# The last chunk's output stores: one SyncE transfer with two row groups in place of a SyncE and a ScalarE transfer

## The chip, the cores and the metric

The kernel runs on one core of a Trainium2 chip (trn2). The metric is the device time of one execution in microseconds, taken as the median over several runs. A profiled execution of its own gives the trace; its span is somewhat shorter than the time of the runs, since it counts from the first to the last instruction.

## The reference

Forgetting attention (causal, with a decay that is the cumulated log of a forget gate), then an MLP with exact gelu over all tokens. Batch 8, heads 8, sequence 576, head size 64, so 4608 tokens of 512 channels; the MLP goes from 512 to 2048 and back.

```python
# q, k, v [8, 8, 576, 64], f [8, 8, 576]; w_in [512, 2048], w_out [2048, 512]
scores = q @ k.T / sqrt(64)
cum = cumsum(log(clip(f, 1e-4, 1.0)))
decay = cum[:, :, :, None] - cum[:, :, None, :]
attn = softmax(where(causal, -1e9, scores + decay)) # "causal" is the part above the diagonal
x = (attn @ v).transpose(0, 2, 1, 3).reshape(4608, 512)
h = x @ w_in
out = (0.5 * h * (1 + erf(h / sqrt(2)))) @ w_out # float32 [4608, 512]
```

## The kernel before

The program works through the 8 batches, each with attention, a first matmul (`gemm1`, 512 to 2048, with gelu on ScalarE) and a second one (`gemm2` and its variants, 2048 to 512). A batch has 576 tokens, but `gemm1` and `gemm2` take 512 tokens at a time, as four blocks of 128 tokens. So the MLP runs over nine chunks: chunks 0 to 7 are the first 512 tokens of each batch, and chunk 8, the last, holds the 64 remaining tokens ("tails") of all eight batches. The tile `tails` collects them.

The order on each engine is that in which the program issues its instructions. For chunks 0 to 6 the second matmul is woven into the attention of a later batch (`gemm2_rows`, `gemm2_half`), and their stores go through `store` (L480 to L481). Chunk 7 and chunk 8 use `gemm2` (L394 on). Lines L728 to L731 are the end of the program: `gemm2` of chunk 7, then sixteen calls of `gemm1` on the tails, then `gemm2` of chunk 8.

In `gemm2` each token block `ts` accumulates sixteen matmuls in one PSUM bank (L408). The last block of chunk 8 is done in two column parts, 384 and then 128 columns (L398 to L403), so that the first part can be copied and stored while the second is computed. When a part is finished, VectorE copies it to an SBUF tile `ot` (L416 to L417). The pool of these tiles, `o_pool`, has four buffers; chunk 8 takes five of them, one for each block and one more for the last block's second part.

The store (L418 to L426) depends on the chunk. In chunks 0 to 7 the 128 tokens of a block are consecutive rows of the output, so it is one transfer on SyncE's queue. In chunk 8 a block of 128 partitions holds the 64 last tokens of one batch and the 64 last tokens of the next. In the output these two groups are 576 rows apart. The kernel before makes two transfers of 64 rows each: partitions 0 to 63 on SyncE's queue, partitions 64 to 127 on ScalarE's. The four blocks give five parts in all (three whole blocks and two column parts), so ten transfers.

`P` is 128, `S` is 576, `TC` is 512, `TL` is 64, `B` is 8, `d_model` is 512.

Of the kernel before, what the change touches and what calls it, by code (L numbers as in the profile page):

```python
# [14 lines left out]
P = 128  # L15
S = 576
# [5 lines left out]
TC = 512  # L22
# [30 lines left out]
def kernel(  # L53
# [10 lines left out]
    nc = tc.nc  # L64
# [8 lines left out]
    TL = S - TC  # L73
# [63 lines left out]
    for t, op, fill in (  # L137
# [4 lines left out]
            out=t[0:D],  # L142
# [251 lines left out]
    def gemm2(c):  # L394

        whole = (0, d_model)
        order = [(ts, kt, whole) for ts in range(n_sub) for kt in range(n_ff)]
        if c == B:  # L398
            order[-n_ff:] = [
                (n_sub - 1, kt, part)  # L400
                for part in ((0, 3 * P), (3 * P, d_model))
                for kt in range(n_ff)
            ]  # L403
        pss = {}
        for ts, kt, (c0, c1) in order:
            if kt == 0:
                pss[ts] = m_psum.tile([P, d_model], FP32, tag="m", name="ps2")
            nc.tensor.matmul(  # L408
                pss[ts][:, c0:c1],
                g_of[c][kt][:, ts * P : (ts + 1) * P],  # L410
                w_out_sb[:, kt, c0:c1],
                start=(kt == 0),
                stop=(kt == n_ff - 1),
            )
            if kt == n_ff - 1:
                ot = o_pool.tile([P, d_model], FP32, tag="ot", name="ot")  # L416
                nc.vector.tensor_copy(ot[:, c0:c1], pss[ts][:, c0:c1])  # L417
                if c < B:  # L418
                    at = [(c * S + ts * P, 0, P)]
                else:  # L420
                    b0 = P // TL * ts
                    at = [(b * S + TC, (b - b0) * TL, TL) for b in range(b0, b0 + P // TL)]
                for row, p0, n in at:
                    (nc.scalar if p0 else nc.sync).dma_start(
                        out[row : row + n, c0:c1], ot[p0 : p0 + n, c0:c1]
                    )  # L426
            yield


# [268 lines left out]
    for b in range(B):  # L698
# [8 lines left out]
        for ffb in range(0 if b > 1 else 4, n_ff):  # L707
# [11 lines left out]
            elif b + 1 < B:  # L719
                first, gap = (5, 3) if b == 1 else (0, 4)  # L720
                at, late = divmod(ffb - first, gap)
# [4 lines left out]
                if ffb == (9 if b == 1 else 14):  # L726
                    load_qk_tokens(b + 2)
    take(gemm2(B - 1), 999)  # L728
    for ffb in range(n_ff):
        gemm1(B, ffb)  # L730
    take(gemm2(B), 999)  # L731


# [28 lines left out]
```

The softmax here doesn't subtract the row's maximum and nothing guards it: scores larger than these inputs give would overflow.

## Time and profile before

| | us |
|---|---|
| median of 3 runs | 345.75 (345.21 to 346.38) |
| span of the profiled execution | 343.4 |
| TensorE busy | 328.6 (96%) |
| ScalarE busy | 212.3 (62%) |
| VectorE busy | 187.0 (54%) |
| GpSimd busy | 124.2 (36%) |
| last gelu on ScalarE begins | 325.9 |
| matmuls of chunk 8's `gemm2` | 325.8 to 339.7 |

Each row of the profile's table of groups is one line of the program on one engine. In the timeline a row has its start in the span, its length, the engine, the line, the operation, the tile written and read, and how many instructions it covers. `SPq` and `ACTq` mark instructions that issue DMAs from SyncE and ScalarE; these aren't counted as busy time. In the DMA view, the lines "DMA" and "GB/s" cut the window into 40 equal slices: a digit is the mean busy share of the core's 16 DMA engines in tenths. The lines of queues below it (q1 is that of SyncE, q10 that of ScalarE) give packets, megabytes, and the time that the packets took as a share of 16 engines over the window. The list of issues gives a transfer's size and its time from issue to landing, that is, to the last of its semaphore increments.

### The profile page before, as it was taken

What the parts mean: (1) busy time and instruction counts of PE and PEld (TensorE: products, weight loads), DVE (VectorE), ACT (ScalarE), POOL (GpSimd) and SP (SyncE); (2) the same over time, 40 slices, a digit from 0 to 9 for tenths busy, and PEclk for the clock granted to TensorE, in tenths of its full rate; (3) what the DMA queues carried; (4) which work ended last, traced back from release to release, by engine and by line L of the source; (5) the groups of instructions that cost most, each with busy time, mean ns of one, the idle gap of its engine ahead of it and who ended that gap; (6) DMA issues with size and microseconds to landing.
All of it is one profiled execution on the core that took longest, in us unless ns stands there. A gap on an engine that the chain in (4) does not pass through costs nothing.

```text
span 343.4 us, 7895 instructions
## 1 busy us (share of the span) xinstructions
PE 328.6 (96%) x3182; PEld 174.7 (51%) x3227; DVE 187.0 (54%) x424; ACT 212.3 (62%) x296; POOL 124.2 (36%) x256
## 2 busy tenths in 40 slices
PE   7799999999999999999999999999999999999995
PEld 3574555445554456545654565446544654444443
DVE  5660355933467935796479646974597542020011
ACT  5986786773644787368746874687468755504600
POOL 8390672228328034543445243714261430000000
PEclk9999999999999999999999999999999999999999
DMA  8999999989993999578945896499900230011013
GB/s 117 178 176 194 201 166 153 170 158 148 237 184 102 139 192 188 82 101 165 211 121 73 141 212 139 71 160 198 169 31 2 65 88 31 2 61 61 0 38 87
DMA packets 99924, 43.03 MB, mean 125 GB/s; under 512 B 78704, under 2 KB 95344, under 8 KB 99888
## 3 DMA queue, kind: packets, MB, share of 16 engines
q1 hardware_dynamic: 82592, 28.37, 41.4%
q0 software_dynamic: 16896, 13.63, 27.2%
q8 instruction: 25, 0.41, 0.5%
q10 hardware_dynamic: 400, 0.52, 0.4%
q14 instruction: 11, 0.09, 0.1%
HBM read 36.85 MB, written 9.44 MB: 135 GB/s over the span
## 4 chain that ended last, share of the span: by engine, by line
PE 89%; issue 2%; POOL 2%; DVE 2%; ACT 2%; DMA 2%; POOLq 0%; ACTq 0%; DVEq 0%
PE ps L375 36%; PE ps L466 25%; PE o L320 9%; PE ps L408 8%; PE s L289 7%; PE ps L501 2%; ACT e L299 2%; DMA k<-in_k_dram 2%; PE ps_x L353 1%; DVE x L334 1%; POOL q L107 1%; PE ps_f L206 1%; POOL k L107 1%; DVE r L333 0%; DVE xT L356 0%
## 5 line engine op out<-in xcount | busy, mean ns | idle before, releaser
L392 ACT ACTIVATE g<-ps 128x512 bf16<-128x512 f32 x144 | 85.3, 597 | 81.1 <-PE ps L375 81.1
L299 ACT ACTIVATE e<-s 128x896 bf16<-128x896 f32 (+2 forms) x128 | 101.2, 836 | 28.5 <-PE s L289 26.8
L375 PE MATMUL ps<-xT,w_in_sb 128*128 128x512 bf16 x497 | 111.4, 379 | 0.8
L466 PE MATMUL ps<-w_out_sb,g 64*128 64x512 bf16 (+1 forms) x731 | 103.0, 376 | 0.8 <-issue 0.8
L375 PEld LDWEIGHTS <-w_in_sb 128*128 128x128 bf16 x576 | 56.0, 98 | 67.5 <-issue 1.8
L301 POOL TENSOR_SCALAR_AFFINE_SELECT e<-e 128x256 bf16<-128x256 bf16 (+1 forms) x135 | 49.2, 383 | 98.9 <-ACT e L299 98.6
L466 PEld LDWEIGHTS <-g 64*128 64x128 bf16 (+1 forms) x756 | 41.5, 94 | 40.4 <-issue 11.9
L244 DVE COPY qT<-tq 64x288 bf16<-64x288 bf16 x96 | 48.7, 507 | 1.4
L289 PE MATMUL s<-qT,kT 64*128 64x320 bf16 (+4 forms) x384 | 45.8, 276 | 3.6 <-ACT e L299 2.7
L260 POOL TENSOR_TENSOR vw<-v_sb,wT 128x640 bf16<-128x640 f32 x31 | 39.6, 1278 | 23.5 <-DMA v_sb<-in_v_dram 23.3
L320 PE MATMUL o<-vw,e 128*128 128x65 bf16 x960 | 36.8, 194 | 3.5 <-issue 2.4
L474 DVE COPY ot<-ps 128x512 f32<-128x512 f32 x26 | 17.9, 689 | 37.1 <-PE ps L466 35.2
L320 PEld LDWEIGHTS <-e 128*128 128x128 bf16 x960 | 34.8, 98 | 5.3 <-PE ps_x L353 0.3
L244 DVE COPY kT<-tk 64x288 bf16<-64x288 bf16 x96 | 33.0, 343 | 1.6
L334 DVE TENSOR_TENSOR x<-o,r 128x320 bf16<-128x320 f32 x64 | 31.4, 491 | 2.4 <-DVE r L333 0.2
L417 DVE COPY ot<-ps 128x512 f32<-128x512 f32 (+2 forms) x9 | 5.7, 632 | 48.8 <-PE ps L408 31.9
L289 PEld LDWEIGHTS <-kT 64*128 64x128 bf16 x384 | 19.5, 94 | 23.2 <-issue 9.7
L408 PE MATMUL ps<-w_out_sb,g 128*128 128x512 bf16 (+2 forms) x142 | 27.9, 355 | 0.1
L333 DVE RECIPROCAL r<-o 128x5 f32<-128x5 f32 x64 | 12.1, 189 | 27.6 <-PE o L320 27.5
L408 PEld LDWEIGHTS <-g 128*128 128x128 bf16 x144 | 13.5, 98 | 14.5
L476 DVE TENSOR_TENSOR ot<-ot,ps 128x512 f32<-128x512 f32 x26 | 17.9, 687 | 1.5
L365 POOL COPY tails<-xT 128x256 bf16<-128x256 bf16 x8 | 3.2, 399 | 31.3 <-DVE xT L356 31.3
(64 smaller groups left out, 158.1 us busy)
## 6 DMA issues: line engine op xcount, KB each, us to landing
out_dram<-ot SPq DMA_DIRECT2D x32, 256.0 KB, 2.3
v_sb<-in_v_dram SPq DMA_DIRECT2D x24, 256.0 KB, 5.3
q<-in_q_dram POOLq DMA_DIRECT2D x6, 576.0 KB, 6.1
k<-in_k_dram POOLq DMA_DIRECT2D x6, 576.0 KB, 8.2
v_sb<-in_v_dram SPq DMA_DIRECT2D x22, 128.0 KB, 5.1
w_in_sb<-in_moe_w_in_dram POOLq DMA_DIRECT2D x4, 512.0 KB, 6.7
w_out_sb<-in_moe_w_out_dram POOLq DMA_DIRECT2D x4, 512.0 KB, 8.4
q<-in_q_dram POOLq DMA_DIRECT2D x4, 144.0 KB, 4.6
```

Source lines behind the costliest of these rows:

```text
L244: nc.vector.tensor_copy(rows[:, odd], src[odd * D : (odd + 1) * D, 2 * i + h].rearrange("d j p -> d p j"),)
L260: eng.tensor_tensor(vw_of[b][:, hs, :, 0:D], v_sb[:, hs, :, :], w.unsqueeze(3).to_broadcast([P, 2, NBLK, D]), Alu.mult,)
L289: nc.tensor.matmul(to, *ab, start=half < 0, stop=half == 1 or not masked)
L299: nc.scalar.activation(et[:, :, z:c], st[:, :, z:c], Act.Exp, scale=scale)
L301: nc.gpsimd.affine_select(out=et[:, :, c0 + z : c0 + P], in_=et[:, :, c0 + z : c0 + P], compare_op=Alu.is_ge, fill=0.0, base=z, pattern=[[ ...
L320: nc.tensor.matmul(o[:, m, :], e_of[b, i, t][:, h, c : c + P], vw_of[b][:, 2 * i + h, n, :], start=(n == 0), stop=(n == m),)
L334: nc.vector.tensor_tensor(x_of[b, i][:, :, h, :], o[:, :, 0:D], r.unsqueeze(2).to_broadcast([P, NBLK, D]), Alu.mult,)
L375: nc.tensor.matmul(ps, w_in_sb[:, kt, ffb * P : (ffb + 1) * P], src[:, kt, 0:TC], start=(kt == 0), stop=(kt == n_dm - 1),)
L392: nc.scalar.activation(g_of[c][ffb], ps, Act.Gelu)
L408: nc.tensor.matmul(pss[ts][:, c0:c1], g_of[c][kt][:, ts * P : (ts + 1) * P], w_out_sb[:, kt, c0:c1], start=(kt == 0), stop=(kt == n_ff - 1),)
L466: nc.tensor.matmul(banks[r], g_of[c][kt][rows, ts * P : (ts + 1) * P], w_out_sb[rows, kt, :], start=kt == (steps.index("r") if r else 0), ...
L474: nc.vector.tensor_copy(ot, banks[1])
```

## The change

The last chunk's store becomes one SyncE transfer for each finished part. Its output side is a view of the output with the batch as a dimension of its own: [2 batches, 64 rows, columns] where the source is [128 partitions, columns]. The transfers of chunks 0 to 7 stay as they were, written in another form.

```diff
                 ot = o_pool.tile([P, d_model], FP32, tag="ot", name="ot")
                 nc.vector.tensor_copy(ot[:, c0:c1], pss[ts][:, c0:c1])
                 if c < B:
-                    at = [(c * S + ts * P, 0, P)]
+                    to = out[c * S + ts * P : c * S + (ts + 1) * P, c0:c1]
                 else:
                     b0 = P // TL * ts
-                    at = [(b * S + TC, (b - b0) * TL, TL) for b in range(b0, b0 + P // TL)]
-                for row, p0, n in at:
-                    (nc.scalar if p0 else nc.sync).dma_start(
-                        out[row : row + n, c0:c1], ot[p0 : p0 + n, c0:c1]
-                    )
+                    to = out.rearrange("(b s) d -> b s d", s=S)[
+                        b0 : b0 + P // TL, TC:S, c0:c1
+                    ]
+                nc.sync.dma_start(to, ot[:, c0:c1])
             yield
```

## The prediction

> **What bounds the kernel now.** I read the chain of waits first, cut to the last 18 us, because every instruction of the change is issued there.
>
> ```profile
> by line: PE ps L408 72.7%; PE ps L375 4.8%; DVE ot L417 1.5%; issue 0.4%
> ...
> 329.11 10.58 PE ps L408 x64
> 339.69 0.02 issue
> 339.71 0.29 DVE ot L417
> ```
>
> Columns are start, length, what. TensorE runs without a gap to 339.69 us, VectorE copies the last 128 columns out of PSUM until 340.00, and the chain stops there: nothing of an engine's own work follows. The span is 343.4 us, so 3.4 us at the end belong to the last stores and the kernel's close. Next the timeline, to see what is issued after that copy, and the list of DMA issues, to see how long it flies.
>
> ```profile
> 340.03 0.48 SPq L424 DMA_DIRECT2D out_dram<-ot  x1
> 340.04 0.76 ACTq L424 DMA_DIRECT2D out_dram<-ot  x1
> ...
> out_dram<-ot SPq DMA_DIRECT2D x1, 32.0 KB, 2.0
> out_dram<-ot ACTq DMA_DIRECT2D x1, 32.0 KB, 2.3
> ```
>
> SyncE's half lands at 340.03 + 2.0 = 342.0 and ScalarE's at 340.04 + 2.3 = 342.3. From 342.3 to 343.4 are 1.1 us of closing work. So the end of the program is: last copy, last landing, 1.1 us. A later last landing moves the end one for one; an earlier one likewise.
>
> Last, the DMA view over single stores. First one of chunk 7 (L424 too, issued at 305.48 as one SyncE transfer of 128 rows, window 306:307.6, slices of 40 ns), then the first pair of the last chunk (window 331.1:332.5, slices of 35 ns).
>
> ```profile
> 305.48 0.33 SPq L424 DMA_DIRECT2D out_dram<-ot  x1
> ...
> DMA  0000000188989896969898987410000000000000
> DMA packets 144, 0.26 MB, mean 164 GB/s; under 512 B 16, under 2 KB 16, under 8 KB 144
> q1 hardware_dynamic: 144, 0.26, 43.7%
> ...
> DMA  0009726999696930929929296997969923100000
> DMA packets 160, 0.26 MB, mean 187 GB/s; under 512 B 32, under 2 KB 32, under 8 KB 160
> q1 hardware_dynamic: 80, 0.13, 45.6%
> q10 hardware_dynamic: 80, 0.13, 24.6%
> ```
>
> Each store is one packet per 2 KB row plus 16 packets under 512 B. The chunk-7 store moves data from 306.31 (eighth slice) to about 307.1, 0.83 us after its issue and for 0.8 us. In the pair, SyncE's queue is q1, ScalarE's q10. q10 was busy 24.6% of 16 engines for 1.4 us, which is 5.51 us for 64 rows: 86 ns of one DMA engine for a 2 KB row. q1 shows 160 ns because its packets share engines with q10's. The whole DMA system is busy 28% of the stretch 329.1 to 339.7, so today these stores are far from any limit.
>
> **What the Trainium skill says.** Of the page "DMA: Bandwidth & Descriptors":
> - Section "Why a DMA increments its semaphore by 16 and not by 1", under how many engines: a transfer is split along the slowest dimension of each access pattern that isn't 1, over the largest number k of engines, at most 16, that divides both sizes; each engine used ends with one semaphore increment. The trace agrees as far as it goes: stores with 128 and with 64 partitions on both sides show 16 small packets each, one for each of 16 engines. No store before has a short slowest dimension, so the trace doesn't show k below 16.
> - Section "Rules for kernel authors": an outermost dimension c below 16 confines a DMA to at most c engines. Not seen before the change.
> - Section "Specifications": about 27 GiB/s for one DMA engine. The trace: 2048 B in 86 ns, 23.8 GB/s, somewhat below.
> - The same rules say that splitting a transfer into two partition halves gains nothing, since both use the same engines. The pair above agrees: 160 ns for a q1 row beside q10.
>
> **The change, part by part.**
> 1. *Removed:* five ScalarE issues (0.5 to 0.76 us each). ScalarE has no other work after its last gelu at 325.92 + 0.60 = 326.5, and nothing is queued behind them but the close. Worth nothing while the stores run; at the end, SyncE's half lands 0.3 us before ScalarE's. So this part alone gives 0 to 0.3 us.
> 2. *Issue on SyncE:* still five DMA issues, each behind the same VectorE copy. Nothing is moved past anything. A 128-row issue takes 0.33 us and its data start 0.83 us later (chunk 7); beside ScalarE it was 0.55 us and 1.2 us (330.03 to 331.24). So the first data come at 330.03 + 0.83 = 330.86, some 0.4 us earlier.
> 3. *The shape.* SBUF's side is 128 partitions. The DRAM side becomes [2 batches, 64 rows, columns]; the batches are 576 rows apart, so the two outer dimensions don't merge. Slowest sizes are 128 and 2, hence k = 2: each DMA engine gets 64 rows, where 16 engines got 8 (4 from each queue). This is where the time goes.
>
> Row prices, on one engine with one queue: 86 ns for 2 KB. For the last token block, a 1536 B row and a 512 B row together: 86 ns if time goes with bytes. The window 340.4:341.8 has q10 at 31.4% of 16 engines for 1.4 us, 7.03 us for 64 such pairs, 110 ns with q1 alongside. I take 92, near the lower end, since q1's competition is in the 110.
> - Each full token block: 64 x 86 ns = 5.5 us. TensorE gives a new one every 3.45 us (copies at 329.31, 332.76, 336.22), so a queue builds up: the first is done at 336.4, the second at 341.9, the third at 347.4. From the first packet on, the two engines never run dry, since each issue (333.5, 336.9, 339.4, 340.0) comes before the previous data are done.
> - Sum for one engine: 64 x (3 x 86 + 92) ns = 22.4 us. Last packet at 330.86 + 22.4 = 353.3.
> - Last packet to landing: data of the last pair ran to about 341.8 and it landed at 342.3, so 0.5 us. Close 1.1 us. End of span 354.9, against 343.4: 11.5 us more.
>
> What else could be hit: the fifth output tile reuses the buffer of the first store (4 buffers), so the last copy, at 339.71, waits until that store has landed, about 336.4 + 0.5 = 336.9. Margin 2.8 us, so the copy stays hidden; without the margin it would still stand behind 8 us of queued stores. TensorE's, VectorE's and gelu work are as before; no other DMA of the program runs after 326 except a few instruction fetches.
>
> The span of 343.4 us is of one profiled execution, 2.35 us below the median of the runs, 345.75; I carry that distance over: 345.75 + 11.5 = 357.2 us.
>
> Bounds for the one unknown, the row on a lonely engine. Low: the page's 27 GiB/s gives, as an estimate, 2048 B in 71 ns and the pair in 71 too; 64 x (3 x 71 + 71) = 18.2 us, so 353.0. High: a store of 8 rows on each engine kept them for 0.83 us of wall clock, 104 ns a row, including the engines' staggered start; with 104 for the pair 26.6 us, so 361.4. I take 86, measured on the same stores, and give some room past either end for the first packet (0.83 or 1.2 us).
>
> **The rivals.**
> - *A: all 16 engines after all* (the transfer is split some other way, on the partitions' side or by rows). The place is the last landing, and the point from which it decides is k: with k = 16, eight rows of 86 ns are 0.7 us a store, no queue builds in 3.45 us, and the last store lands 2.0 us after issue instead of 2.3. End 343.1, so 345.5 us: no measurable change, and not slower. For it: the plain stores all show 16 small packets. Against: the page, twice, and no store with a short dimension in the trace. A sub-case with over 1 us gained would need the close to shrink as well, since ScalarE has no transfer left to wait for; the 1.1 us of close is work of all engines after the last landing, so this is faint.
> - *B: two engines, but no queue*, because a lonely engine is much faster than 86 ns. It decides at 3.45 us / 64 = 54 ns a row. Then only the last store's own length counts: at 50 ns, the 1536 B rows of the fourth block take 64 x 38 = 2.4 us from 340.2 to 342.6, the 512 B rows 64 x 13 = 0.8 us, landing 343.9, end 345.0: 347.4 us. Against it: q10's rows were 86 ns when the DMA system was partly idle.
> - *C: two engines, and a long run of writes on one engine is slower than the eight rows seen so far*, say at the 160 ns of q1's rows: 64 x (3 x 160 + 160) = 41.0 us, end 373.5, so 375.8 us. Against: those 160 ns are two queues in turn, 2 x 80. For: no store in the trace shows more than 8 rows in a row on one engine.
>
> **How the numbers follow.** Forecast (k = 2 at about 86 ns a row) 0.80; A 0.10, with 0.02 more for its faster sub-case; B 0.03; C 0.05. A measurement of this kernel tells 0.3%, 1.0 us, from no change. Slower: 0.80 + 0.03 + 0.05 = 0.88; same 0.10; faster 0.02. The forecast's own range is 352 to 363 (353.0 and 361.4 with the room for the start); it holds the 0.80, so the range ends there, and all rivals lie outside.
>
> **What would show it.** In the changed kernel's profile: a store's DMA window with 128 rows and 2 small packets instead of 16 (step 3), the DMA share near 2/16 = 0.125 from about 331 to 353 with some 45 to 48 GB/s, rows of about 86 ns (share x 16 x time / rows), TensorE's last matmul still at 339.7, and times to landing that climb from store to store: about 6.9 us for the first, then 8.9, 11.0, 12.6 and 13.8 for the last. Wrong if small packets stay at 16 per store (A), if landings don't climb (B), or if the DMA share is 0.125 for over 30 us (C). If the last copy is later than 340, the reuse of the output buffer was mispriced.

## The result, and the profile after

The changed kernel takes 357.9 us (median of 4 runs, 357.61 to 359.12), the kernel before 345.73 in the same comparison. The ratio is 1.0355, 95% interval 1.0335 to 1.0376. The forecast was 357.2.

The profiled execution's span went from 343.4 to 355.6 us. The same views as before, in the same order. First the chain of waits of the changed kernel, from 325 us on (start, length, what):

```profile
by line: PE ps L408 44.7%; PE ps L375 3.6%; DVE ot L417 0.9%; issue 0.1%
...
339.90 0.02 issue
339.92 0.29 DVE ot L417
```

The computation is hardly later: the last copy begins at 339.92 where it began at 339.71. What lies after it has grown from 343.4 - 339.71 = 3.7 us to 355.6 - 339.92 = 15.7 us. That accounts for 12.0 of the 12.2 us that the span gained. This stretch, from the start of the last copy to the end of the span, is the measure used for all runs below ("the tail"), since it leaves out what an execution gained or lost earlier.

Next the five store issues of the changed kernel, from the timeline, each asked for by itself:

```profile
330.24 0.67 SPq L425 DMA_DIRECT2D out_dram<-ot  x1
...
333.69 0.54 SPq L425 DMA_DIRECT2D out_dram<-ot  x1
...
337.15 0.51 SPq L425 DMA_DIRECT2D out_dram<-ot  x1
...
339.62 0.51 SPq L425 DMA_DIRECT2D out_dram<-ot  x1
...
340.25 4.83 SPq L425 DMA_DIRECT2D out_dram<-ot  x1
```

They come right behind the copies, as before. The last one takes 4.83 us to issue, where issues took 0.3 to 0.8 before. Last, the DMA view of the changed kernel over the whole time in which its stores move data (slices of 0.555 us), and busy time in three stretches of it (the last three columns are the granted TensorE clock, the DMA share and GB/s):

```profile
GB/s 30 30 30 30 37 41 48 52 52 52 52 52 52 52 48 52 48 52 52 52 52 52 52 52 52 52 52 52 52 47 50 50 53 50 50 50 50 42 43 33
DMA packets 650, 1.05 MB, mean 47 GB/s; under 512 B 10, under 2 KB 266, under 8 KB 650
q1 hardware_dynamic: 650, 1.05, 13.1%
```

```profile
331.50:337.80 6.30, 6.30 (x33) 3.12 (x32) 1.38 (x2) 0.00 (x0) 0.00 (x0) 1.00 0.13 42
337.80:348.00 10.20, 2.08 (x24) 1.47 (x21) 0.85 (x2) 0.00 (x0) 0.00 (x0) 0.82 0.13 51
348.00:353.50 5.50, 0.00 (x0) 0.00 (x0) 0.00 (x0) 0.00 (x0) 0.00 (x0) 0.50 0.13 48
```

Read three things there. There are 650 packets: 640 rows (five parts of 128) and 10 small ones, two a store instead of 16 a queue and store. The DMA share is 0.13, about 2/16, and it stays there without a gap until 353.5. And the rate sits at 50 to 52 GB/s, that is 25 to 26 GB/s for each of two DMA engines, while the first slices are at 30. The tail is the time in which two engines finish moving a megabyte. The clock is 1.00 while TensorE works and lower only in the stretches that reach past its last matmul at 339.9, so it has no part in the loss.

### The profile page after: what moved, and what is told of

Same layout as the page of the kernel before. It is cut to its first block, busy times and chain, and to the rows that moved or that the text cites. A ratio compares the mean times of both kernels' runs of the same rounds, so it can differ in the third digit from the quotient of the medians.

```text
span 355.6 us, 7929 instructions
## 1 busy us (share of the span) xinstructions
PE 334.2 (94%) x3227; PEld 174.6 (49%) x3227; DVE 186.7 (52%) x424; ACT 212.4 (60%) x296; POOL 124.5 (35%) x256
## 4 chain that ended last, share of the span: by engine, by line
PE 87%; POOL 2%; DVE 2%; ACT 2%; DMA 2%; issue 1%; POOLq 0%; ACTq 0%; DVEq 0%
PE ps L375 35%; PE ps L465 26%; PE o L320 8%; PE ps L408 8%; PE s L289 7%; PE ps L500 2%; ACT e L299 2%; DMA k<-in_k_dram 2%; PE ps_x L353 1%; DVE x L334 1%; POOL q L107 1%; PE ps_f L206 1%; POOL k L107 1%; DVE r L333 0%; DVE xT L356 0%
## 5 line engine op out<-in xcount | busy, mean ns | idle before, releaser
L465 PE MATMUL ps<-w_out_sb,g 64*128 64x512 bf16 (+1 forms) x756 | 110.2, 377 | 0.0
L375 PE MATMUL ps<-tails,w_in_sb 128*128 128x512 bf16 x64 | 14.4, 378 | 0.0
```

Of the source, the lines that this page charges most:

```text
L375: nc.tensor.matmul(ps, w_in_sb[:, kt, ffb * P : (ffb + 1) * P], src[:, kt, 0:TC], start=(kt == 0), stop=(kt == n_dm - 1),)
L465: nc.tensor.matmul(banks[r], g_of[c][kt][rows, ts * P : (ts + 1) * P], w_out_sb[rows, kt, :], start=kt == (steps.index("r") if r else 0), ...
```

## The experiments

Unless said otherwise each edit is made to the changed kernel, and each ratio is to runs of the kernel before that were taken beside it. Tails can be told apart to about 0.3 us: the kernel before and the two kernels below whose last parts are stored as in it have tails of 3.5 to 3.8 us.

**64 groups of two rows instead of two groups of 64.** The transfer stays one SyncE transfer with a two-level output side; only the order of its dimensions is turned, and the tails are interleaved to match.

```diff
-        nc.gpsimd.tensor_copy(tails[:, :, b * TL : (b + 1) * TL], xT(b)[:, :, XC - TL :])
+        to = tails.rearrange("p k (t r u) -> p k t u r", t=n_sub, u=P // TL)
+        nc.gpsimd.tensor_copy(to[:, :, b // 2, b % 2], xT(b)[:, :, XC - TL :])
-                    to = out.rearrange("(b s) d -> b s d", s=S)[
-                        b0 : b0 + P // TL, TC:S, c0:c1
+                    to = out.rearrange("(b s) d -> s b d", s=S)[
+                        TC:S, b0 : b0 + P // TL, c0:c1
```

> Still one SyncE transfer a part, but the tails are interleaved so that the output side is [64 rows, 2 batches, columns]: 16 divides both slowest sizes, 64 and 128. Theory (the short outer dimension confines the transfer to two DMA engines): the loss is gone, span 343.0 to 343.9 us, ratio to the kernel before 0.998 to 1.002, 16 small packets a store. Rival (a single SyncE transfer, or any two-level output side, is slow in itself, whatever the outer size): stays near 355 us, ratio 1.03.

Measured: 345.65 us against 345.59, ratio 1.0008 (0.9981 to 1.0035); tail 343.6 - 339.57 = 4.0 us. Its first store in the DMA view (window 330.9 to 332.3):

```profile
DMA packets 144, 0.26 MB, mean 187 GB/s; under 512 B 16, under 2 KB 16, under 8 KB 144
q1 hardware_dynamic: 144, 0.26, 49.9%
```

Sixteen small packets are back, the busy share of the window is half of 16 engines, and the loss is gone. So the single transfer, SyncE's queue and the two-level output side are all innocent. It is also the form in which a single SyncE transfer costs nothing that the runs can tell; it brings nothing measurable either.

**Two transfers, both on SyncE.**

```diff
-                nc.sync.dma_start(to, ot[:, c0:c1])
+                for p0 in (0,) if c < B else (0, TL):
+                    nc.sync.dma_start(
+                        to if c < B else to[p0 // TL],
+                        ot[:, c0:c1] if c < B else ot[p0 : p0 + TL, c0:c1],
+                    )
```

> Two transfers of 64 rows each, as in the kernel before, but both on SyncE. Theory: 16 engines each, so only the second issue is later, by about 0.5 us, and lands near 342.5: span 343.4 to 344.0, ratio 0.999 to 1.003. Rival (it is ScalarE's queue that the kernel before needs): several us slower, ratio over 1.01.

Measured: 346.6 us against 345.59, ratio 1.0033 (1.0012 to 1.0055); tail 344.6 - 339.89 = 4.7 us, 1.0 more than before. The issues at the end, from the timeline:

```profile
339.58 1.11 SPq L426 DMA_DIRECT2D out_dram<-ot  x2
...
341.13 1.11 SPq L426 DMA_DIRECT2D out_dram<-ot  x2
```

The last copy ends at 339.89 + 0.29 = 340.18, but SyncE is issuing the pair before it until 340.69 and begins the last pair at 341.13; in the kernel before that began at 340.03. So it isn't ScalarE's queue as such that the kernel before needs, but a second engine that issues: four issues in a row on SyncE cost about 1 us at the end of the program, just above what was expected (1.003). Nor is the order of the output rows the cause of the 12 us: these ten transfers write the rows of the changed kernel to the same places, from the same queue. What fills the 0.44 us between 340.69 and 341.13 stays open.

**Eight groups of 16 rows, and four groups of 32.** The tails are reordered so that a block holds 16 rows of every batch, or 32 rows of four batches. The store of the first and of the second:

```diff
+                    r = P // B
-                        b0 : b0 + P // TL, TC:S, c0:c1
+                        :, TC + ts * r : TC + (ts + 1) * r, c0:c1
```

```diff
+                    r0 = TC + TL // 2 * (ts % 2)
-                        b0 : b0 + P // TL, TC:S, c0:c1
+                        B // 2 * (ts // 2) : B // 2 * (ts // 2 + 1),
+                        r0 : r0 + TL // 2,
+                        c0:c1,
```

> One SyncE transfer with output side [8 batches, 16 rows, columns], tails reordered to match. Theory: 8 engines, 16 rows each, 1.3 us a block, no queue; the last two parts take 1.0 and 0.4 us from about 340.6: span 343.5 to 344.3, ratio 1.000 to 1.003, 8 small packets a store. Rival (more groups cost more, by group): slower than the two-group kernel, over 355 us.

> One SyncE transfer with output side [4 batches, 32 rows, columns], tails reordered to match. Theory: 4 engines, 32 rows each, 2.6 us a block, still under the 3.45 us between blocks, so no queue builds; the last two parts take 1.95 and 0.8 us from about 340.6: span 344.8 to 345.6, ratio 1.003 to 1.007, 4 small packets a store. Rival (loss in proportion to rows an engine, without a threshold): half of the 12 us, near 349, ratio 1.017.

Measured with eight groups: 347.01 us, ratio 1.0048 (1.0029 to 1.0067), tail 345.1 - 340.10 = 5.0 us. With four: 349.79 us, ratio 1.0119 (1.0083 to 1.0154), tail 350.4 - 342.42 = 8.0 us. The order is as the theory has it (64 groups 4.0, eight 5.0, four 8.0, two 15.7 us of tail), and the small packets are 8 and 4 a store. But both are dearer than expected. The DMA view of a first store each, eight groups (window 331.7 to 334.3, slices of 65 ns), then the first part of that of four groups (334 to 336, slices of 50 ns) and its rest (336 to 338.8, which also holds the beginning of the next store):

```profile
GB/s 0 158 158 32 126 63 0 95 32 32 32 32 32 0 32 95 63 32 63 32 189 189 252 126 221 126 221 189 189 189 189 221 189 158 126 126 0 32 0 0
DMA packets 136, 0.26 MB, mean 101 GB/s; under 512 B 8, under 2 KB 8, under 8 KB 136
```

```profile
DMA packets 32, 0.07 MB, mean 33 GB/s; under 512 B 0, under 2 KB 0, under 8 KB 32
...
DMA packets 116, 0.23 MB, mean 82 GB/s; under 512 B 4, under 2 KB 4, under 8 KB 116
```

With eight groups the first 1.3 us run far below the rate of some 190 GB/s that the store then has (8 x 24). With four groups 32 rows move in the first 2 us, where four engines at the predicted 86 ns a row would do 93. These stores have a slow start that the expectation did not have. For four groups that lifts a block from 2.6 us to about 4 (334.0 to 338.1), more than the 3.45 us between blocks, so a queue builds up after all, and the threshold that the theory put between four groups and two is crossed at four. Neither the expected 1.003 to 1.007 nor the rival's 1.017 came out.

**Which of the five stores matter.** Two kernels with the two-group transfer for one part alone; all others stored as in the kernel before, on SyncE and ScalarE. For block 0 alone:

```diff
-                nc.sync.dma_start(to, ot[:, c0:c1])
+                if c < B or ts == 0:
+                    nc.sync.dma_start(to, ot[:, c0:c1])
+                else:
+                    nc.sync.dma_start(to[0], ot[0:TL, c0:c1])
+                    nc.scalar.dma_start(to[1], ot[TL:P, c0:c1])
```

> Two groups in one SyncE transfer for block 0 of the last chunk alone; the other four parts as in the kernel before. Theory: block 0 needs two engines until about 337.8, and the later rows that queue behind it on those two still land before 340 or so; the end isn't touched: span 343.2 to 343.8, ratio 0.999 to 1.002. Rival (each two-group store costs its own time, 12 us / 5): about 345.8, ratio 1.007.

Measured: 345.84 us against 345.87, ratio 1.0006 (0.9986 to 1.0027), and a tail of 347.4 - 343.64 = 3.8 us. (The span of this profile is long because its last copy is late, at 343.64; the median of its runs is that of the kernel before.) Two engines for one block cost nothing as long as matmuls cover them.

For the last 128 columns alone the condition is `c1 - c0 == P` instead of `ts == 0`.

> Two groups in one SyncE transfer for the last 128 columns alone; the other four parts as before. Theory: 64 rows of 512 B in turn on two engines, 64 x 24 ns = 1.5 us instead of 0.2, all of it uncovered: span 344.4 to 345.2, ratio 1.003 to 1.006. Rival (only the queue of the big blocks matters): 343.4, ratio 1.000.

Measured: 346.46 us against 345.87, ratio 1.0008 (0.999 to 1.0025); tail 344.7 - 339.88 = 4.8 us, 1.1 more than before. Its last stores in the DMA view, window 341.4 to 343.3:

```profile
q1 hardware_dynamic: 130, 0.07, 11.7%
q10 hardware_dynamic: 33, 0.03, 4.5%
```

The trace shows the expected run of rows on two engines and the later end in that execution. The comparison of runs doesn't confirm it: the interval lies below the expected 1.003 and includes no change. The medians are 0.6 us apart and the fastest runs 1.1 (345.92 and 344.80), which speaks for a small loss rather than none; its size stays open. So the last part alone is worth at most 0.25%, and the loss of the change is, for the most part, the queue of the blocks in front of it.

**Two queues.** The changed kernel's five transfers, issued in turn on SyncE and ScalarE.

```diff
-                nc.sync.dma_start(to, ot[:, c0:c1])
+                eng = nc.scalar if c == B and (ts % 2 or c0) else nc.sync
+                eng.dma_start(to, ot[:, c0:c1])
```

> All five parts with two groups as in the change, but issued in turn on SyncE and ScalarE. Theory (two DMA engines are the bound): the same bytes on the same two engines, span 354 to 356, ratio 1.030 to 1.037, rows of about 160 ns where both queues have work. Rival (SyncE's one queue is the bound, and each queue brings its own engines or its own rate): about 348, ratio 1.013.

Measured: 357.58 us against 345.87, ratio 1.0334 (1.031 to 1.0359); tail 355.3 - 339.53 = 15.8 us. ScalarE's first issue, from the timeline, and the DMA view in the windows 331 to 337 and 337 to 345:

```profile
333.31 1.14 ACTq L426 DMA_DIRECT2D out_dram<-ot  x1
```

```profile
q1 hardware_dynamic: 119, 0.24, 12.8%
...
DMA packets 207, 0.41 MB, mean 51 GB/s; under 512 B 4, under 2 KB 15, under 8 KB 207
...
q10 hardware_dynamic: 141, 0.28, 9.0%
q1 hardware_dynamic: 66, 0.13, 4.2%
```

Two queues move the same 51 GB/s, and the tail is that of the changed kernel. Both queues use the same two engines, and those are the bound, not SyncE's queue. The part of the expectation on rows of 160 ns fell. At first the queues don't meet: q10 has not one packet before 337, though ScalarE issued at 333.31, and SyncE's second store, issued at 336.75, moves its first rows at about 340.5. From 341 on the queues take turns, and still a row costs what it did before. In the window 345 to 347:

```profile
q1 hardware_dynamic: 28, 0.06, 7.3%
q10 hardware_dynamic: 28, 0.04, 5.7%
```

Both have 28 packets there, and one of q1's 2 KB rows takes 7.3% x 16 x 2 us / 28 = 83 ns.

**The number of engines without a batch dimension.** Here the kernel before is the base, and two stores of chunk 7 are cut by partitions, both sides plain rows.

```diff
-                    at = [(c * S + ts * P, 0, P)]
+                    n = {0: 122, 3: 124}.get(ts, P) if c == B - 1 else P
+                    row = c * S + ts * P
+                    at = [(row, 0, n)] + [(row + n, n, P - n)] * (n < P)
-                    (nc.scalar if p0 else nc.sync).dma_start(
+                    (nc.scalar if p0 and c == B else nc.sync).dma_start(
```

> The kernel before with two stores of chunk 7 cut by partitions, both sides plain rows and no batch dimension: block 0 as 122 and 6 rows, block 3 as 124 and 4, all on SyncE. Theory (the number of DMA engines is the largest up to 16 that divides the slowest sizes): block 0 uses 2 engines with 61 rows (2 small packets) and then 6 with one row each, done some 6 us after its data start; block 3 uses 4 engines with 31 rows and then 4 with one, 2.6 to 4.5 us; the slow start of about 1 us seen in the two-, four- and eight-group kernels shows too, since it goes with few engines. All of it is hidden by the matmuls of chunks 7 and 8: ratio 0.998 to 1.002. Rival (the two-level output side is what confines and slows the transfer): 16 engines or nearly so, data moved within 0.9 us of their start.

Measured: 345.5 us against 346.19, ratio 0.9983 (0.9961 to 1.0005); tail 343.6 - 340.11 = 3.5 us. Block 3 in the DMA view, window 313.4 to 318, slices of 115 ns:

```profile
GB/s 0 53 71 71 53 18 36 36 0 0 36 0 36 53 89 89 53 89 71 53 53 71 71 89 89 107 107 89 125 71 89 89 53 53 53 53 36 53 18 0
DMA packets 136, 0.26 MB, mean 57 GB/s; under 512 B 8, under 2 KB 8, under 8 KB 136
```

124 and 4 rows leave 8 small packets, as 4 + 4 engines would, and the 128 rows take over 4 us, where they took 0.8 in chunk 7 before. Of block 0 (122 and 6 rows) only 50 rows moved in the 3 us from 303 to 306. So few engines and the slow start come with the sizes of the slowest dimensions, not with the two-level view of the output. And the runs don't notice, since matmuls cover it.

## Why the prediction was right

The mechanism is shown, not only argued: give the same transfer an outer size that 16 divides and the loss goes; give it two queues and it stays; cut plain rows into 124 and 4 and the few engines appear elsewhere. Step by step:

- *Removed ScalarE issues, and the issue on SyncE* (0 to 0.3 us gained). Right in that it is too small to measure: one SyncE transfer on 16 engines is at 1.0008 (0.9981 to 1.0035). That it is a gain isn't shown; its tail is 0.3 us longer, not shorter. With two transfers a part, sharing their issue between SyncE and ScalarE is worth about 1 us against both on SyncE.
- *k = 2.* Right: two small packets a store, DMA share 0.13. This came from the Trainium skill's page "DMA: Bandwidth & Descriptors", section "Why a DMA increments its semaphore by 16 and not by 1", and no store of the kernel before could show it; the runs agree for outer sizes of 2, 4, 8 and 64, and for plain rows of 124 with 4.
- *The queue.* Right that blocks of over 5 us meet a block every 3.45 us and that the engines don't run dry. The trace gives no times to landing for these stores, so the climb that the prediction named as a sign is read from the data: the first store's end at 337.8, the second's near 343.0, the third's near 348.1 and the fifth's at 353.5, which is 7.6, 9.3, 11.0 and 13.2 us after their issues. The reuse of the output buffer stayed hidden, as predicted: the last copy starts right behind the last matmul.
- *Row prices.* 86 ns was a little high for the steady state. At 51 GB/s on two engines a 2 KB row comes every 2048 / 25.5 = 80 ns, while one packet lasts 83 (13.0% x 16 x 5 us / 126 packets, window 340 to 345), so the packets overlap slightly. The last two parts took 5.4 us (348.1 to 353.5), 84 ns for a pair of rows instead of 92. The 160 ns of a q1 row beside q10, which the prediction put down to two queues in turn, did not come back where two queues did take turns (83 ns); what stretched those rows stays open.
- *First data and first block.* Too low. The data start 331.5 - 330.24 = 1.3 us after the issue, not 0.83, and the first block runs until 337.8, 6.3 us instead of 5.5, through the slow start. Since the queue never empties afterwards, the changed kernel pays this only once.
- *The sum of the busy stretch.* 353.5 - 331.5 = 22.0 us against 22.4: the slow start (0.8 us too little) and the cheaper rows (1.2 us too much) nearly cancel. That is luck.
- *Landing and close.* From the end of the last packets to the end of the span 355.6 - 353.5 = 2.1 us, not 1.6.

Together the span came to 355.6 where the sum gave 354.9: 0.2 us because TensorE was later in this execution, 0.4 from the later start of the data, minus 0.4 from the busy stretch, plus 0.5 from the close. The distance of 2.35 us from span to median held (357.9 - 355.6 = 2.3). So the mechanism carried the forecast to within its range, and the closeness of 357.2 to 357.9 owes something to errors of opposite sign.

Of the rivals, 16 engines after all and two engines without a queue are out by the DMA share and the 22 us. The rival of a long run of writes being slower than short ones is out as well: after the first block the rows got faster, not slower.

## What to carry to other kernels

When two transfers are merged into one by adding a dimension, look at the size of the outermost dimension on both sides before counting saved issues: two groups of 64 rows ran on two DMA engines, 64 groups of two rows on sixteen, with the same bytes. If the data's layout can be chosen (here the order of the tails), choose it so that 16 divides the outer size (64 was tried here). How much few engines cost is a question of cover: one such store was free in front of 10 us of matmuls; a queue of them at the end of the program made up most of 12 us.

## What was not expected of the hardware

- Transfers on two, four and eight engines start slowly: 30 GB/s instead of 51 in the first 2 us with two engines, 33 GB/s in the first 2 us with four, and about 1.3 us far below rate with eight. A store on 16 engines shows nothing like it: all its data move within 0.8 us. What causes this wasn't tried.
- With two queues on the same two engines, a store issued while another was under way began late: 333.31 to 337.1 on ScalarE's queue, 336.75 to about 340.5 on SyncE's, some 3.8 us each, where the changed kernel's first store needed 1.3. It did not wait for the other store's end the second time, since from 341 on the two took turns. What delays it wasn't tried.
- An issue can itself be held up: the fifth store behind a long queue kept SyncE for 4.83 us, and ScalarE's first one in the kernel with two queues took 1.14. Nothing was queued behind them here; what it would do to a transfer there wasn't tried.
